# Reducing an angle in place in PSUM, and moving the split of a rotation's products between engines

## The chip, the cores and the metric

The kernel runs on one core of a Trainium2 chip. The metric is the device time of one execution in microseconds (us); of several runs the median counts. The core's engines are named as in the profile: PE (TensorE, matmul; PEld is its weight load), DVE (VectorE), ACT (ScalarE), POOL (GpSimd) and SP (SyncE, which issues the DMAs). Each engine works through its own instructions in order, and waits at an instruction until what that one needs is there. SBUF is the on-chip memory that all engines reach. PSUM is the memory that PE writes to, in 8 banks of 128 x 512 float32. In this kernel GpSimd only touches SBUF.

## The reference

Cut to what matters here; before it stands a clustered attention over 2 batches, 8 heads and 768 tokens, whose result is `x` of 2 x 768 x 512.

```
x = x + (relu(x.T @ w_tok1) @ w_tok2).T        # mixes tokens
x = x + relu(x @ w_ch1) @ w_ch2                # mixes channels, width 1536
theta = x @ w_theta                            # the rotation
zr, zi = x * cos(theta), x * sin(theta)
y = w_tok_r @ zr + w_tok_i @ zi                # over the tokens of one batch
u = x + y
out = u + relu(u @ w_ch)
```

Inputs are float32 or float64, and the products are kept to float32 accuracy.

## The kernel before

Every float32 operand of a product is split into two parts of the type float32r, x = h + l. One product is then three matmuls, l*h, h*l and h*h (`mm3`, L116 to L122), and each operand that is made on the chip has to be split first: h is a copy of x, l is x - h. `split_ps` (L86) splits from PSUM, with the copy on ACT and the subtraction on DVE. `split_sb` (L75) splits from SBUF with the engines that its last two arguments name: the copy by POOL ("p"), DVE ("v") or ACT ("a"), the subtraction by POOL ("p") or DVE ("v").

Tokens stand in 12 tiles of 128, six of each batch; `xn[t]` is tile t, 128 x 512, in SBUF. After the attention come the channel mixing and the rotation. The last third of the channel width (from L666) goes in three groups `ch` of four token tiles. For a group, `up` is called four times and `down` once for each of its tiles, and `advance()` is called after each of these, which is a tick. On these ticks a list `plan` runs the rotation of tiles that are done: `x2_turn(t)` transposes the tile and splits it, two ticks later `theta(t)` multiplies it by w_theta into a PSUM bank and `angle(t)` follows, one tick later `trig(t)`, and one more later `products(t)`. `up` ends with a split by ACT (L623) and DVE (L624), and `down` with an addition to `xn[t]` on DVE (L631), which `x2_turn` of that tile needs.

The angle is reduced by its whole turns before the sine. `angle` computes n = theta / 2 pi + MAGIC on ACT (L593), takes MAGIC off on DVE (L594), which leaves a rounded integer, and subtracts n times 2 pi in two steps on DVE (L595, L596), from PSUM into an SBUF tile r. `trig` takes |r| on ACT (L603), clips r on DVE (L604), and takes two sines on ACT (L605 for the cosine, L606 for the sine). `products` multiplies both by `xn[t]` and splits them: the cosine with DVE (L613), DVE (L80) and POOL (L84), the sine with POOL (L613), ACT (L82) and DVE (L84).

The last phase goes by `mix(t, b)`: 36 matmuls over the twelve split products z of one batch's six tiles, then an addition to xn on DVE (L698). One step later `u3_turn` transposes and splits the result, and a step after that `finish` multiplies it by w_ch and stores. The order of the steps begins (0,0), (1,0), (0,1), (2,0): the third is the first that needs tiles 6 to 11. `load_w` brings in each weight piece in between: a DMA, two ACT, two DVE (L105, L106) and a POOL instruction (L109), and a split whose subtraction is on POOL (L84).

PSUM banks of this part come from one pool of 8 (`bank`); SBUF tiles for the angle come from a pool of 8 with the tag "trig". The order of the instructions on each engine is set by the compiler, which simulates the program when it lays out the queues; the order in the source is the priority.

Of the kernel before, what the change touches and what calls it, by code (L numbers as in the profile page):

```python
# [18 lines left out]
P = 128  # L19
# [6 lines left out]
# How each chunk of the turned softmax is split: A by ScalarE and VectorE, B with GpSimd's difference, C by  # L26
# ScalarE's copy and GpSimd.
# [19 lines left out]
ZR = "va"  # L47
ZS = "pv"
# [3 lines left out]
def tile_model(ctx: ExitStack, tc: tile.TileContext, qT, kT, v, cent, w1, w2, wc1, wc2, wth, wri, wch, out):  # L52
    """Every float32 operand of a product is split exactly, x = h + l, into two float32r parts of 12
    significant bits; h*h + h*l + l*h are three one-pass products, accumulated in float32."""
    nc = tc.nc
    B, H, D, S = qT.shape
    NT = S // P          # token tiles of one batch
    NH = S // 2          # half of a row of scores: one PSUM bank
# [4 lines left out]
    NTT = w2.shape[1]    # tiles of the token-mixing width  # L63
# [10 lines left out]
    # ---------------------------------------------------------------- splits  # L74
    def split_sb(h, l, x, rnd, sub):  # L75
        """h, l <- x (SBUF), by the engines named."""
        if rnd == "p":
            nc.gpsimd.tensor_scalar(out=h, in0=x, scalar1=1.0, scalar2=0.0, op0=ALU.mult, op1=ALU.add)
        elif rnd == "v":
            nc.vector.tensor_copy(out=h, in_=x)  # L80
        else:
            nc.scalar.activation(out=h, in_=x, func=AF.Copy)  # L82
        e = nc.gpsimd if sub == "p" else nc.vector
        e.tensor_tensor(out=l, in0=x, in1=h.bitcast(F32), op=ALU.subtract)  # L84
# [8 lines left out]
    def load_w(src, name, pool=None):  # L93
        """A piece of a weight, [128, 512] float64, rounded to float32 and split."""
        raw = wpool.tile([P, 512, 2], U32, tag="wraw", bufs=3, name=f"{name}_raw")
        nc.sync.dma_start(out=raw.rearrange("p n t -> p (n t)"), in_=src.bitcast(U32))
        lo, hi = raw[:, :, 0], raw[:, :, 1]
        # The high word as a float32 has 3 bits of the exponent in its fraction; times 2^-112 is its
        # exponent in float32's bias. Shifted by 3 those fields are float32's, and the low word's top
        # bits, rounded, complete the fraction.  # L100
        w = wpool.tile([P, 512], F32, tag="wf", bufs=2, name=f"{name}_f")
        nc.scalar.activation(out=w, in_=hi.bitcast(F32), func=AF.Copy, scale=2.0**-112)
        nc.scalar.activation(out=lo, in_=lo, func=AF.Copy, scale=2.0**-29)
        wu = w.bitcast(U32)
        nc.vector.tensor_scalar(out=hi, in0=wu, scalar1=3, scalar2=None, op0=ALU.logical_shift_left)  # L105
        nc.vector.scalar_tensor_tensor(  # L106
            out=wu, in0=wu, scalar=0x80000000, in1=hi, op0=ALU.bitwise_and, op1=ALU.bitwise_or
        )
        nc.gpsimd.tensor_tensor(out=wu, in0=wu, in1=lo, op=ALU.add)  # L109
        pool, n = (pool, 12) if pool else (blk, WG)  # L110
        h, l = (pool.tile([P, 512], F32R, tag="wg", bufs=n, name=f"{name}_{k}") for k in "hl")
        split_sb(h, l, w, "pa"[wcount[0] % 2], "p")
        wcount[0] += 1
        return h, l

    def mm3(ps, pairs, first, last):  # L116
        """ps (+)= sum over the split pairs (lhsT, rhs) of lhsT.T @ rhs."""
        n = len(pairs)
        for i, ((ah, al), (bh, bl)) in enumerate(pairs):
            nc.tensor.matmul(ps, ah, bl, start=first and i == 0, stop=False)  # L120
            nc.tensor.matmul(ps, al, bh, start=False, stop=False)  # L121
            nc.tensor.matmul(ps, ah, bh, start=False, stop=last and i == n - 1)  # L122

    # ------------------------------------------------------------- attention
    with ExitStack() as actx:
# [10 lines left out]
        # Products of zeros keep the tensor engine's clock up.  # L136
# [8 lines left out]
        # Normalized centroids, placed for the products with two heads at a time.  # L145
# [9 lines left out]
        # One Newton step makes the root exact to float32.  # L155
# [9 lines left out]
        # cst[:, pair, 96 + 16 j + c]: two heads' centroids. The 128 columns from 96 - 32 i place their  # L165
        # products in rows 32 i ..
# [18 lines left out]
        # ltri.T @ x: of each row, the sum of the rows before it in its block of 16  # L185
# [12 lines left out]
        # one-hot rows of queries stay, those of keys become 0 (same cluster) or -BIG  # L198
# [11 lines left out]
        def masks(b, pr):  # L210
            """Cluster rows of two heads, 16 j .. for head j: one-hot of the queries' halves in rows 0 .. and
            32 .., of the keys' in 64 .. and 96 .. In steps, to go between other work."""
# [11 lines left out]
            # The factor 1 / (|q| + eps) of a row is positive and moves no maximum over the clusters.  # L224
# [17 lines left out]
            # Of equal maxima the first counts: the one with none before it.  # L242
# [26 lines left out]
        def prep_first(b, h):  # L269
            """Operands of a head: scores = [qh; qh].[kh; kl] + [ql; one-hot].[kh; mask]."""  # L270
# [35 lines left out]
        def split_pair(b, pr, ts):  # L306
            """Two heads' queries and keys, split."""
            parts = []
            for x, f, k in zip(ts, (scale, 1.0), "qk"):
                hi, lo = (ap.tile([P, S], F32R, tag="hl", bufs=HL, name=f"{k}{j}{b}{pr}") for j in "hl")  # L310
                if f != 1.0:
                    nc.gpsimd.tensor_scalar(out=x, in0=x, scalar1=f, scalar2=0.0, op0=ALU.mult, op1=ALU.add)
                split_sb(hi, lo, x, "p", "p")
                parts += [hi, lo]
            pairs[b, pr] = parts
# [3 lines left out]
        def place(i, m):  # L319
            """The cluster rows of head i of a pair."""  # L320
# [7 lines left out]
        def prep(b, h, m):  # L328
            """Operands of a head: scores = [qh; qh].[kh; kl] + [ql; one-hot].[kh; mask]."""
# [16 lines left out]
        def scores(b, h, u, ops):  # L346
            """Two tiles of queries: their softmax's numerators."""
# [22 lines left out]
        def turn(b, h, u, es):  # L370
            """Numerators with the keys on partitions, split."""
# [23 lines left out]
        def values(b, h, u, pr, vs):  # L395
            """[vh | vl].T @ (ph + pl); the halves' sum is the head's output, transposed."""
# [15 lines left out]
        def tokens(b, half):  # L412
            """x += relu(x.T @ w1) @ w2 for half of the channels, in 12 pieces."""
# [43 lines left out]
        def natural(b, pr):  # L457
            """Two heads' output with the tokens on partitions, divided by the softmax's sums."""
# [95 lines left out]
    # ------------------------------------------------------------------ mixers  # L554
    # channels: u + relu(u @ wc1) @ wc2
# [19 lines left out]
    def x2_turn(t):  # L575
        """x2 with the channels on partitions, split."""
        ps = bank(f"x2t{t}")
        for c in range(NC):
            nc.tensor.transpose(ps[:, c * P : c * P + P], xn[t][:, c * P : c * P + P], ident)
        h, l = block(f"x2h{t}"), block(f"x2l{t}")  # L580
        split_ps(h, l, ps)
        x2s[t] = h, l
# [6 lines left out]
    def angle(t):  # L589
        """theta less its whole turns."""  # L590
        th = ths.pop(t)
        n, r = (blk.tile([P, 512], F32, tag="trig", bufs=8, name=f"{k}{t}") for k in "nr")
        nc.scalar.activation(out=n, in_=th, func=AF.Copy, scale=INV2PI, bias=MAGIC)  # L593
        nc.vector.tensor_scalar(out=n, in0=n, scalar1=-MAGIC, scalar2=None, op0=ALU.add)  # L594
        nc.vector.scalar_tensor_tensor(out=r, in0=n, scalar=-C1, in1=th, op0=ALU.mult, op1=ALU.add)  # L595
        nc.vector.scalar_tensor_tensor(out=r, in0=n, scalar=-C2, in1=r, op0=ALU.mult, op1=ALU.add)  # L596
        trigs[t] = r

    def trig(t):
        """The angle's cosine, sin(pi/2 - |r|), and sine."""  # L600
        r = trigs[t]
        ra = blk.tile([P, 512], F32, tag="trig", bufs=8, name=f"ra{t}")
        nc.scalar.activation(out=ra, in_=r, func=AF.Abs)  # L603
        nc.vector.tensor_scalar(out=r, in0=r, scalar1=PI_LO, scalar2=-PI_LO, op0=ALU.min, op1=ALU.max)  # L604
        nc.scalar.activation(out=ra, in_=ra, func=AF.Sin, bias=halfpi, scale=-1.0)  # L605
        nc.scalar.activation(out=r, in_=r, func=AF.Sin)  # L606
        trigs[t] = ra, r

    def products(t):
        """x2's products with the cosine and the sine, split."""  # L610
        z = []
        for k, (tr, e) in enumerate(zip(trigs.pop(t), (nc.vector, nc.gpsimd))):
            e.tensor_tensor(out=tr, in0=tr, in1=xn[t], op=ALU.mult)  # L613
            zh, zl = block(f"zh{t}{k}"), block(f"zl{t}{k}")
            split_sb(zh, zl, tr, ZR[k], ZS[k])
            z.append((zh, zl))
        zs[t] = z
# [25 lines left out]
    # The last of the channels' width goes by groups of token tiles, with the rotation of the groups  # L643
    # that are done in between.
# [39 lines left out]
    # tokens again, then u + relu(u @ wch)  # L684
# [95 lines left out]
```

## Time and profile before

| What | Value |
|---|---|
| Runs, us | 704.73, 708.43, 709.75 (median 708.43) |
| Profiled execution: span, us | 707.2 |
| PE busy, us (share of the span) | 664.1 (94%) |
| DVE busy | 467.5 (66%) |
| POOL busy | 394.9 (56%) |
| ACT busy | 361.3 (51%) |
| HBM over the span | 62 GB/s |

The profile has no time of its own for the profiled execution but its span, from the first to the last instruction; it lies 1.2 us below the median of the runs and within their spread. Busy shares are means over the whole span: the attention, the channel mixing, the rotation and the last mixing have different loads, and rows of a stretch are read below.

### The profile page before, as it was taken

The page shows a single profiled execution, that of the slowest core. Times are in us where ns is not written, and L with a number is a line of the kernel's source. Part 1 is how long each engine was busy: PE and PEld are TensorE (multiplying, and loading weights), DVE is VectorE, ACT ScalarE, POOL GpSimd, SP SyncE. Part 2 cuts the span into 40 slices and gives each one's busy share as a digit, 9 for nine tenths or more (in the row PEclk, how much of TensorE's full clock was granted, in tenths as well). Part 3 has the DMA queues.
Part 4 walks back from the last instruction along what each step waited for, and adds up shares of the span by engine and source line. Part 5 has one row for each costly group of instructions (what it writes and reads, how often), then busy time and mean ns, then how long its engine had stood idle before and what let it go on. Part 6 is the DMA issues. An engine that isn't in the chain of part 4 may idle for free.

```text
span 707.2 us, 10584 instructions
## 1 busy us (share of the span) xinstructions
PE 664.1 (94%) x3772; PEld 580.9 (82%) x3772; DVE 467.5 (66%) x734; ACT 361.3 (51%) x698; POOL 394.9 (56%) x376
## 2 busy tenths in 40 slices
PE   7898888989999999999999999999996968999998
PEld 4798788888999999888888888888885846888886
DVE  6889888868788878376664432449799996433122
ACT  3687878687868786255533420435565444321000
POOL 7977789586838563348865520604476777433000
PEclk9999999999999999999999999999998999999999
DMA  8645645485434500013442310300011313320001
GB/s 259 159 89 156 172 106 144 100 246 141 90 85 104 121 19 1 1 50 130 150 149 60 120 59 1 107 14 1 31 44 45 93 55 109 101 89 16 31 30 45
DMA packets 24533, 62.27 MB, mean 88 GB/s; under 512 B 4320, under 2 KB 7584, under 8 KB 24480
## 3 DMA queue, kind: packets, MB, share of 16 engines
q1 hardware_dynamic: 24480, 61.59, 31.4%
q8 instruction: 30, 0.49, 0.3%
q14 instruction: 23, 0.19, 0.1%
HBM read 40.44 MB, written 3.15 MB: 62 GB/s over the span
## 4 chain that ended last, share of the span: by engine, by line
PE 71%; DVE 14%; DMA 4%; ACT 3%; issue 3%; SPq 2%; POOL 2%; ACTq 0%; DVEq 0%; POOLq 0%
PE o L401 7%; PE t L378 6%; PE r L120 4%; PE r L121 4%; PE r L122 4%; PE c L121 4%; PE c L122 4%; PE c L120 4%; PE y L120 4%; PE y L121 4%; PE y L122 4%; PE s L356 4%; PE s L357 3%; DMA w_raw<-w 3%; PE po L120 2%
## 5 line engine op out<-in xcount | busy, mean ns | idle before, releaser
L361 DVE TENSOR_REDUCE nm<-s 128x1 f32<-128x768 f32 x96 | 90.9, 948 | 18.0 <-PE s L357 17.4
L363 ACT ACTIVATE e<-s,nm 128x768 f32<-128x768 f32 x96 | 86.9, 905 | 22.4 <-DVE nm L361 11.8
L378 PE MATMUL t<-ident,e 128*128 128x128 f32 x576 | 81.6, 277 | 6.4 <-DVE pl L88 5.2
L356 PE MATMUL s<-k,qh 128*128 128x384 f32 x192 | 70.8, 369 | 8.6 <-ACT e L363 6.3
L401 PE MATMUL o<-ph,vs 128*128 128x256 f32 x288 | 76.0, 295 | 2.5 <-DVE xt L408 2.5
L378 PEld LDWEIGHTS t<-ident,e 128*128 128x128 f32 x576 | 68.7, 143 | 11.5 <-DVE pl L88 4.9
L401 PE MATMUL o<-pl,vs 128*128 128x256 f32 x288 | 73.6, 288 | 0.0
L88 DVE TENSOR_TENSOR pl<-t,ph 128x512 fp32r<-128x512 f32 x96 | 62.9, 678 | 6.7 <-ACT ph L87 5.1
L357 PE MATMUL s<-k,q 128*128 128x384 f32 x192 | 65.9, 344 | 1.3 <-ACT k L254 1.3
L87 ACT ACTIVATE ph<-t 128x512 fp32r<-128x512 f32 x96 | 54.9, 598 | 19.6 <-PE t L378 16.0
L389 POOL TENSOR_TENSOR pl<-pr,ph 128x512 fp32r<-128x512 f32 x48 | 62.7, 1306 | 2.0
L388 POOL TENSOR_SCALAR ph<-pr 128x512 fp32r<-128x512 f32 x48 | 30.6, 638 | 56.5 <-ACT pr L384 50.4
L401 PEld LDWEIGHTS o<-ph,vs 128*128 128x128 f32 x288 | 54.9, 191 | 3.9 <-DVE xt L408 3.5
L120 PE MATMUL y<-zl,k_h 128*128 128x512 f32 x144 | 56.9, 397 | 0.0
L121 PE MATMUL y<-zh,k_l 128*128 128x512 f32 x144 | 56.8, 394 | 0.0
L120 PE MATMUL r<-ul,c_h 128*128 128x512 f32 x144 | 56.7, 394 | 0.0
L121 PE MATMUL c<-c_h,rl 128*128 128x512 f32 x144 | 56.4, 393 | 0.2 <-DVE rl L624 0.2
L122 PE MATMUL y<-zh,k_h 128*128 128x512 f32 x144 | 56.5, 392 | 0.0
L122 PE MATMUL c<-c_h,rh 128*128 128x512 f32 x144 | 56.4, 393 | 0.0
L121 PE MATMUL r<-uh,c_l 128*128 128x512 f32 x144 | 56.0, 389 | 0.0
L120 PE MATMUL c<-c_l,rh 128*128 128x512 f32 x144 | 56.0, 396 | 0.0
L122 PE MATMUL r<-uh,c_h 128*128 128x512 f32 x144 | 55.9, 389 | 0.0
(201 smaller groups left out, 1718.1 us busy)
## 6 DMA issues: line engine op xcount, KB each, us to landing
c_raw<-wc SPq DMA_DIRECT2D x24, 512.0 KB, 3.4
k_raw<-wri SPq DMA_DIRECT2D x18, 512.0 KB, 3.7
qh<-qh SPq DMA_DIRECT2D x28, 192.0 KB, 3.0
k<-kh SPq DMA_DIRECT2D x28, 192.0 KB, 3.8
ql<-qT SPq DMA_DIRECT2D x8, 384.0 KB, 4.2
kl<-kT SPq DMA_DIRECT2D x8, 384.0 KB, 4.5
vr<-v SPq DMA_DIRECT2D x16, 192.0 KB, 3.2
w_raw<-w SPq DMA_DIRECT2D x6, 512.0 KB, 4.3
```

Of the source, the lines that this page charges most:

```text
L87: nc.scalar.activation(out=h, in_=ps, func=AF.Copy)
L88: nc.vector.tensor_tensor(out=l, in0=ps, in1=h.bitcast(F32), op=ALU.subtract)
L120: nc.tensor.matmul(ps, ah, bl, start=first and i == 0, stop=False)
L121: nc.tensor.matmul(ps, al, bh, start=False, stop=False)
L122: nc.tensor.matmul(ps, ah, bh, start=False, stop=last and i == n - 1)
L356: nc.tensor.matmul(ps[:, half, :NH], qh[:, c], k1[:, n], start=True, stop=False)
L357: last = nc.tensor.matmul(ps[:, half, :NH], ql[:, c], kk[:, n], start=False, stop=True)
L361: nc.vector.tensor_reduce(out=nm, in_=ps[:, :, :NH], axis=AX.XY, op=ALU.max, negate=True)
L363: nc.scalar.activation(out=e.rearrange("p (a n) -> p a n", a=2), in_=ps[:, :, :NH], func=AF.Exp, bias=nm, accum_out=sums[b, h // 2][:, qt, ...
L378: nc.tensor.transpose(ps[:, a, i * P : i * P + P], es[i][:, kt * P : kt * P + P], ident)
L389: nc.gpsimd.tensor_tensor(out=pl, in0=raw, in1=ph.bitcast(F32), op=ALU.subtract)
L401: nc.tensor.matmul(ps[:, :256], vs[:, kt, :], p[:, kt % 2, :], start=n == 0 and k == 0, stop=n == NT - 1 and k == 1,)
```

## The change

The angle is no longer brought to an SBUF tile. MAGIC is taken off on ACT. Both subtractions write back into theta's own PSUM bank, |r| and the clip read from there, and the first of the two sines, the cosine, is written over it. DVE multiplies the cosine by x2 in the bank, and `split_ps` splits it from there: copy on ACT, subtraction on DVE. The bank is held until that subtraction has read it. The sine keeps its product on POOL and its copy on ACT; its subtraction goes from DVE to POOL, and the cosine's subtraction from POOL to DVE. Comments are dropped as well; nothing else is changed.

```diff
     def angle(t):
-        th = ths.pop(t)
-        n, r = (blk.tile([P, 512], F32, tag="trig", bufs=8, name=f"{k}{t}") for k in "nr")
+        th = ths[t]
+        n = blk.tile([P, 512], F32, tag="trig", bufs=8, name=f"n{t}")
         nc.scalar.activation(out=n, in_=th, func=AF.Copy, scale=INV2PI, bias=MAGIC)
-        nc.vector.tensor_scalar(out=n, in0=n, scalar1=-MAGIC, scalar2=None, op0=ALU.add)
-        nc.vector.scalar_tensor_tensor(out=r, in0=n, scalar=-C1, in1=th, op0=ALU.mult, op1=ALU.add)
-        nc.vector.scalar_tensor_tensor(out=r, in0=n, scalar=-C2, in1=r, op0=ALU.mult, op1=ALU.add)
-        trigs[t] = r
+        nc.scalar.activation(out=n, in_=n, func=AF.Copy, bias=-MAGIC)
+        nc.vector.scalar_tensor_tensor(out=th, in0=n, scalar=-C1, in1=th, op0=ALU.mult, op1=ALU.add)
+        nc.vector.scalar_tensor_tensor(out=th, in0=n, scalar=-C2, in1=th, op0=ALU.mult, op1=ALU.add)

     def trig(t):
-        r = trigs[t]
-        ra = blk.tile([P, 512], F32, tag="trig", bufs=8, name=f"ra{t}")
-        nc.scalar.activation(out=ra, in_=r, func=AF.Abs)
-        nc.vector.tensor_scalar(out=r, in0=r, scalar1=PI_LO, scalar2=-PI_LO, op0=ALU.min, op1=ALU.max)
-        nc.scalar.activation(out=ra, in_=ra, func=AF.Sin, bias=halfpi, scale=-1.0)
+        th = ths.pop(t)
+        ra, r = (blk.tile([P, 512], F32, tag="trig", bufs=8, name=f"{k}{t}") for k in ("ra", "r"))
+        nc.scalar.activation(out=ra, in_=th, func=AF.Abs)
+        nc.vector.tensor_scalar(out=r, in0=th, scalar1=PI_LO, scalar2=-PI_LO, op0=ALU.min, op1=ALU.max)
+        nc.scalar.activation(out=th, in_=ra, func=AF.Sin, bias=halfpi, scale=-1.0)
         nc.scalar.activation(out=r, in_=r, func=AF.Sin)
-        trigs[t] = ra, r
+        trigs[t] = th, r

     def products(t):
-        z = []
-        for k, (tr, e) in enumerate(zip(trigs.pop(t), (nc.vector, nc.gpsimd))):
-            e.tensor_tensor(out=tr, in0=tr, in1=xn[t], op=ALU.mult)
-            zh, zl = block(f"zh{t}{k}"), block(f"zl{t}{k}")
-            split_sb(zh, zl, tr, ZR[k], ZS[k])       # ZR = "va", ZS = "pv"
-            z.append((zh, zl))
-        zs[t] = z
+        co, r = trigs.pop(t)
+        (ch, cl), (sh, sl) = ((block(f"z{j}{t}{k}") for j in "hl") for k in range(2))
+        nc.vector.tensor_tensor(out=co, in0=co, in1=xn[t], op=ALU.mult)
+        split_ps(ch, cl, co)
+        nc.gpsimd.tensor_tensor(out=r, in0=r, in1=xn[t], op=ALU.mult)
+        split_sb(sh, sl, r, "a", "p")
+        zs[t] = [(ch, cl), (sh, sl)]
```

## Rows read from the trace of the kernel before

**Rows 1.** Busy us by stretch: length, PE, PEld, DVE, ACT, POOL; then granted clock, DMA.

```profile
480.00:500.00 20.00, 20.00 (x92) 16.41 (x92) 18.17 (x27) 10.45 (x18) 9.59 (x7) 1.00 0.00 1
...
515.00:531.50 16.50, 16.35 (x72) 13.08 (x71) 16.43 (x20) 8.96 (x17) 11.68 (x9) 1.00 0.20 64
531.50:541.40 9.90, 4.07 (x13) 3.22 (x12) 9.16 (x13) 3.95 (x7) 5.93 (x5) 0.66 0.17 53
541.40:571.40 30.00, 30.00 (x138) 24.50 (x136) 27.09 (x33) 16.45 (x30) 22.95 (x17) 1.00 0.23 70
571.40:589.30 17.90, 8.62 (x30) 6.89 (x30) 15.52 (x18) 8.16 (x15) 14.02 (x10) 0.81 0.21 60
...
600.00:640.00 40.00, 40.00 (x186) 33.15 (x185) 15.74 (x23) 11.12 (x18) 18.68 (x17) 1.00 0.29 89
```

**Rows 2.** Timeline of PE: start us, us, instruction, then idle before it and releaser.

```profile
537.59 1.12 PE L579 MATMUL x2t<-ident,xn 128*128 128x128 f32 x4 [5.83 <-DVE xn L631]
...
541.42 0.39 PE L121 MATMUL c<-c_h,rl 128*128 128x512 f32 x1
541.64 0.39 PE L122 MATMUL c<-c_h,rh 128*128 128x512 f32 x1
...
546.58 0.60 PE L579 MATMUL x2t<-ident,xn 128*128 128x128 f32 x4
546.94 0.47 PE L120 MATMUL th<-th_l,x2h 128*128 128x512 f32 x1
...
575.57 1.12 PE L703 MATMUL u<-ident,xn 128*128 128x128 f32 x4 [4.11 <-DVE xn L698]
...
578.97 0.40 PE L120 MATMUL y<-zl,k_h 128*128 128x512 f32 x1
...
586.36 1.12 PE L703 MATMUL u<-ident,xn 128*128 128x128 f32 x4 [5.17 <-DVE xn L698]
...
589.28 0.39 PE L120 MATMUL y<-zl,k_h 128*128 128x512 f32 x1
```

**Rows 3.** Timeline of DVE from 515 us: an early instruction and two additions.

```profile
515.64 0.68 DVE L88 TENSOR_TENSOR x2l<-x2t,x2h 128x512 fp32r<-128x512 f32 x1
...
536.86 1.28 DVE L631 TENSOR_TENSOR xn<-c,xn 128x512 f32<-128x512 f32 x2
...
574.84 0.68 DVE L698 TENSOR_TENSOR xn<-y,xn 128x512 f32<-128x512 f32 x1
```

**Rows 4.** Groups of DVE by line, 466 to 590 us: count, busy us, mean ns.

```profile
L84 DVE TENSOR_TENSOR zl<-r,zh 128x512 fp32r<-128x512 f32 x12 | 15.5, 1296 | 2.5 <-ACT zh L82 2.5
L613 DVE TENSOR_TENSOR ra<-ra,xn 128x512 f32<-128x512 f32 x12 | 14.3, 1191 | 2.0 <-ACT ra L605 1.9
L596 DVE SCALAR_TENSOR_TENSOR r<-n,r 128x512 f32<-128x512 f32 x12 | 10.9, 908 | 0.3
L594 DVE TENSOR_SCALAR n<-n 128x512 f32<-128x512 f32 x12 | 9.8, 816 | 3.8 <-ACT n L593 3.8
L80 DVE CAST zh<-ra 128x512 fp32r<-128x512 f32 x12 | 8.4, 703 | 0.1
L604 DVE TENSOR_SCALAR r<-r 128x512 f32<-128x512 f32 x12 | 8.0, 665 | 1.4 <-ACT ra L603 1.4
```

**Rows 5.** Single lines, 466 to 590 us: shortest, median and longest in ns.

```profile
L594 DVE TENSOR_SCALAR n<-n x12: 411/424/1536, 472.0 to 569.3; 128x512 f32<-128x512 f32 x12
...
L595 DVE SCALAR_TENSOR_TENSOR r<-n,th x12: 671/677/690, 473.1 to 571.3; 128x512 f32<-128x512 f32 x12
...
L613 DVE TENSOR_TENSOR ra<-ra,xn x12: 676/1104/1798, 477.8 to 579.2; 128x512 f32<-128x512 f32 x12
L613 POOL TENSOR_TENSOR r<-r,xn x12: 1287/1583/1746, 478.3 to 580.4; 128x512 f32<-128x512 f32 x12
...
L84 POOL TENSOR_TENSOR zl<-ra,zh x12: 1268/1404/1695, 482.8 to 585.1; 128x512 fp32r<-128x512 f32 x12
```

**Rows 6.** Groups of ACT by line, 466 to 590 us: count, busy us, mean ns.

```profile
L82 ACT ACTIVATE zh<-r 128x512 fp32r<-128x512 f32 x12 | 7.5, 624 | 9.6 <-POOL r L613 9.6
...
L87 ACT ACTIVATE x2h<-x2t 128x512 fp32r<-128x512 f32 x11 | 6.5, 593 | 3.1 <-PE x2t L579 3.1
```

More of the change, by code (lines that the diff above doesn't have):

```diff
@@ L46 @@
 WARM = (17, 4, 20, 18)
-ZR = "va"
-ZS = "pv"
 @with_exitstack
@@ L589, in angle @@
     def angle(t):
-        th = ths.pop(t)
-        n, r = (blk.tile([P, 512], F32, tag="trig", bufs=8, name=f"{k}{t}") for k in "nr")
-        nc.scalar.activation(out=n, in_=th, func=AF.Copy, scale=INV2PI, bias=MAGIC)
-        nc.vector.tensor_scalar(out=n, in0=n, scalar1=-MAGIC, scalar2=None, op0=ALU.add)
-        nc.vector.scalar_tensor_tensor(out=r, in0=n, scalar=-C1, in1=th, op0=ALU.mult, op1=ALU.add)
-        nc.vector.scalar_tensor_tensor(out=r, in0=n, scalar=-C2, in1=r, op0=ALU.mult, op1=ALU.add)
@@ L597, in angle @@
-        trigs[t] = r
-    def trig(t):
-        r = trigs[t]
-        ra = blk.tile([P, 512], F32, tag="trig", bufs=8, name=f"ra{t}")
-        nc.scalar.activation(out=ra, in_=r, func=AF.Abs)
-        nc.vector.tensor_scalar(out=r, in0=r, scalar1=PI_LO, scalar2=-PI_LO, op0=ALU.min, op1=ALU.max)
-        nc.scalar.activation(out=ra, in_=ra, func=AF.Sin, bias=halfpi, scale=-1.0)
+        th = ths[t]
+        n = blk.tile([P, 512], F32, tag="trig", bufs=8, name=f"n{t}")
+        nc.scalar.activation(out=n, in_=th, func=AF.Copy, scale=INV2PI, bias=MAGIC)
@@ new lines, in angle, with trig @@
+        nc.scalar.activation(out=n, in_=n, func=AF.Copy, bias=-MAGIC)
+        nc.vector.scalar_tensor_tensor(out=th, in0=n, scalar=-C1, in1=th, op0=ALU.mult, op1=ALU.add)
+        nc.vector.scalar_tensor_tensor(out=th, in0=n, scalar=-C2, in1=th, op0=ALU.mult, op1=ALU.add)
+    def trig(t):
+        th = ths.pop(t)
+        ra, r = (blk.tile([P, 512], F32, tag="trig", bufs=8, name=f"{k}{t}") for k in ("ra", "r"))
+        nc.scalar.activation(out=ra, in_=th, func=AF.Abs)
+        nc.vector.tensor_scalar(out=r, in0=th, scalar1=PI_LO, scalar2=-PI_LO, op0=ALU.min, op1=ALU.max)
+        nc.scalar.activation(out=th, in_=ra, func=AF.Sin, bias=halfpi, scale=-1.0)
```

## The prediction

> **What bounds the kernel now.** I read the busy times first. PE is busy for 664.1 of 707.2 us, so the place to look is where it isn't. Busy times by stretch show that inside the rotation: PE is full up to 531 us, then has 4.07 of 9.90 us and 8.62 of 17.90 us in two stretches around a full one, and is full again afterwards [rows 1]. The timeline of PE says what it waits for. Three times it stands before a group of transposes: 5.83 us for the addition of L631, 4.11 us and 5.17 us for that of L698 [rows 2]. That is 15.11 us. Each addition is one DVE instruction of under 0.7 us that only needs a finished matmul; it is late because DVE has other work queued ahead of it. DVE is busy for 16.43 of 16.50 us, 9.16 of 9.90, 27.09 of 30.00 and 15.52 of 17.90 us in these stretches, while ACT and POOL have room [rows 1]. So in this part DVE's queue sets the end.
>
> After each wait PE also runs slower for a while: the granted clock of the two stretches with waits is 0.66 and 0.81, against 1.00 in the full ones, which is a mix of the two levels, 1.2 and 2.4 GHz [rows 1]. From 537.59 to 541.42 us it starts a group of four transposes and seven matmuls. At full clock the transposes take 0.36 us (546.58 to 546.94) and a matmul starts every 0.23 us (541.42 to 541.64), so this should be 0.36 + 7 x 0.23 = 1.97 us; it is 3.83, and 1.86 us is lost. After the second wait (575.57 to 578.97, six matmuls) it is 3.40 - 1.74 = 1.66 us, after the third (586.36 to 589.28, five) 2.92 - 1.51 = 1.41 us [rows 2]. In all 4.93 us. **The waits and the slow clock behind them are worth 15.11 + 4.93 = 20.0 us.** No other stall of PE in the rotation or the last mixing is as long, and DVE is 90% busy at 480 to 500 us as well, with PE full [rows 1], so work that DVE saves there buys nothing.
>
> Why DVE is so slow shows in the spread of single lines. L595, which reads theta in PSUM, takes 671 to 690 ns in all twelve cases. L594 has both operands in SBUF and takes 411 to 1536 ns, L613 with two SBUF inputs 676 to 1798 [rows 5]. DVE's SBUF work is stretched while POOL works, its PSUM work isn't.
>
> **DVE's part.** Per tile DVE now spends 1.296 + 1.191 + 0.908 + 0.816 + 0.703 + 0.665 us on L84, L613, L596, L594, L80 and L604 [rows 4] and 0.677 on L595 [rows 5]: 6.26 us. The change leaves two subtractions, the clip, the cosine's product and its l part: five instructions, each with one PSUM input. I price each at 0.677 us, the median of L595: 3.39 us. **DVE saves 2.87 us per tile.** Three of the five now write to PSUM, which no row of DVE shows. Its cost lies between 0.671 us, the shortest of L595 (a shorter one is not expected, since the shortest two-input row with everything in SBUF is 0.676), and twice the price, 1.354 us, should read and write in one bank exclude each other [rows 5]. I take the lower end, because the nearest row already streams the same 512 elements from PSUM.
>
> The saving against the three waits:
> - First wait. Between L88 at 515.64 and L631 at 536.86 us [rows 3] DVE runs almost without a pause, and 17 of its instructions there are the rotation's, at seven per tile 2.4 tiles. 2.4 x 2.87 = 6.9 us, so L631 starts at 530.0. PE arrives at 537.59 - 5.83 = 531.8 [rows 2]. The wait goes, with 1.8 us to spare.
> - Second wait. Up to L698 at 574.84 [rows 3] there are 21 such instructions from 541.4 us on, three tiles: 8.6 us, so 566.2. PE arrives at 571.5. The wait goes.
> - Third wait. By then all four last tiles are through, 11.5 us. The second L698 ends just before 586.36 and moves to about 575, PE arrives at 581.2. The wait goes.
>
> **ACT's part.** It gets two copies more per tile: MAGIC from SBUF at the price of L82, 0.624 us, and the cosine's h from PSUM at that of L87, 0.593 [rows 6]: 1.22 us, 4.9 us for the last four tiles. From 541.4 to 589.3 us it is busy for 24.6 of 47.9 us [rows 1], so the copies lie beside DVE's and PE's work. The cosine overwrites what the clip reads, so the sine of L605 now waits for DVE's clip. Behind it in ACT's queue stand the other sine, x2h, rh and the weights' copies; DVE, PE and POOL wait for those. If that cover is gone, the chain of a tile grows by the 1.22 us and as many as two handovers.
>
> **POOL's part.** Product and subtraction of the sine take the place of product and subtraction of one each: the count is the same, 1.58 + 1.40 us by the medians of its rows, with shortest ones of 1.287 and 1.268 [rows 5]. But the sine's way is now POOL, ACT, POOL, with a copy of 0.624 us [rows 6] for which POOL stands still if nothing else is queued. POOL is busy for 22.95 + 14.02 = 37.0 of the 47.9 us from 541.4 to 589.3 [rows 1]. Without the waits of PE that stretch lasts some 40 us, of which POOL fills 37. The stall that remains is therefore POOL's: between nothing and about 6 us, when its idle time of 10.9 us is kept to the half. I take 2.5 us, nearer to nothing, because POOL's own work is stretched too and shortens when DVE leaves SBUF. No DMA is added or moved; the loads behind these POOL instructions only follow their buffers.
>
> **The bank.** Theta's bank is now held until the cosine's l part is written, instead of until L595. Six instructions more of 0.6 to 0.7 us and their handovers make about 5 us, plus what they queue. The pool of eight covers it at the pace of one tile per 24 matmuls and a group of transposes, 24 x 0.23 + 0.36 = 5.9 us.
>
> **A rule against it.** The rows price an addition of a constant at 411 ns on DVE when undisturbed, 816 ns on average [rows 4, 5], and a copy on ACT at 624 [rows 6]. The Trainium skill, "ScalarE: Activation LUTs", Rules for kernel authors, says that additions and the like belong on VectorE and not on ScalarE; by it the move of MAGIC would cost 0.2 us of engine time per tile. The trace agrees only for an undisturbed DVE.
>
> **Sum.** 20.0 us less 2.5 us that remain: 17.5 us. The profiled span of 707.2 becomes 689.7 us; the median of the runs lies 1.2 us higher, 708.43 - 17.5 = 690.9. **I forecast 691 us.**
>
> **The rivals.**
> - POOL becomes the bound: it keeps its gaps, and the last tiles' sines and the next weights come about 6 us late, with some 1.5 us of slow clock behind, and perhaps a second time for less. 20 - 10 = 10 us gained: 698 us. For it: 37 of 40 us. Against it: only the sine needs POOL now.
> - PSUM writes are dear, 1.354 us for three instructions. The saving falls to 0.84 us per tile: L631 comes at 534.8 (3.0 us of the wait remain), the two L698 about 1 us late each, and the clock's 4.9 us stay: 20 - 9.9 = 10 us, 698 us.
> - The stretching stays with DVE. If POOL's accesses hold up DVE as long as before, only at other instructions (L105, L106), what counts is the undisturbed price: three at the 0.411 us of the shortest L594 and four at 0.677 [rows 5] are 3.94 us, a saving of 0.55 per tile. Then 4.5, 2.4 and 2.9 us of the waits and all of the clock's cost remain, 5.3 us are gained: 703 us. The Trainium skill, "VectorE: DVE Perf Modes", Rules for kernel authors, points this way: who has many operations to do on a matmul's output should copy it out of PSUM first. Against it: L595 isn't stretched once in twelve.
> - Slower: PE runs out of banks. If so many banks hold angles that each group of matmuls has to wait for the evacuation of the one before, ACT 0.593 and DVE 0.677 us [rows 5, 6], the some 30 groups of this part lose 30 x 1.27 = 38 us: 691 + 38 = 729 us. This begins when six of eight banks hold angles, at a hold of 6 x 5.9 = 35 us in the even part. The new chain needs about a quarter of that; only the last four tiles, whose thetas follow each other closely, come near, with two mixes and a transpose beside them.
> - The compiler lays the queues out anew, and the additions stand behind other work again: no change, 708 us.
>
> **How the numbers follow.** Forecast 0.63 (687 to 695), POOL 0.14, dear writes 0.07, stretching stays 0.06, out of banks 0.05, no change 0.05. The runs before spread by 0.7%, so a change of 1% is about what can be told: faster is below 701.3 us, slower above 715.5. Faster: 0.63 + 0.14 + 0.07 and a part of the stretching, 0.86; same 0.09; slower 0.05. The range goes from 686 us (all 20 us gained, and a run at the low end of the spread) to 702.
>
> **What would show it.** After the change PE's idle time before L579 and L703 should be below 1 us each and the granted clock 1.00 throughout these stretches; the five DVE lines should stand at 0.67 to 0.69 us with almost no spread; DVE should be busy for about two thirds of the stretch and POOL for over 85%; L698 should start within 1 us of its matmul. The prediction is wrong if PSUM writes show above 0.8 us, if PE waits with a release from POOL's l parts or from a bank, or if DVE stays over 90% busy with L105 and L106 stretched.

## The result and the profile after

The changed kernel takes 690.99 us in the median of 4 runs (689.80 to 692.06), against 708.69 us of 4 runs before. The ratio is 0.9759, with a 95% interval of 0.9725 to 0.9792. The forecast was 691. The profiled execution spans 690.2 us, 17.0 us less than before. Two constants went and `angle` got a line shorter, so the lines behind them have lower numbers now: the addition of `down` is L628 (it was L631), that of `mix` L695 (L698), the transposes L577 and L700 (L579 and L703), `split_ps` L85 and L86.

Busy times by stretch of the changed kernel, with the columns of [rows 1]:

```profile
515.00:531.50 16.50, 16.50 (x77) 13.68 (x76) 14.42 (x24) 14.13 (x26) 12.48 (x11) 1.00 0.30 95
531.50:541.40 9.90, 8.30 (x44) 6.71 (x43) 7.36 (x10) 7.49 (x14) 7.70 (x8) 1.00 0.01 2
541.40:571.40 30.00, 28.35 (x129) 22.97 (x128) 22.75 (x34) 23.21 (x42) 25.20 (x21) 1.00 0.36 105
571.40:589.30 17.90, 17.90 (x82) 14.83 (x81) 10.77 (x14) 5.76 (x10) 13.68 (x12) 1.00 0.41 127
```

PE has 4.07 of 9.90 and 8.62 of 17.90 us no more [rows 1], but 8.30 and 17.90, and the granted clock of these stretches is 1.00 instead of 0.66 and 0.81. DVE comes down from 27.09 to 22.75 us in the long stretch, ACT rises from 16.45 to 23.21, POOL from 22.95 to 25.20 because more of its work now falls into that stretch.

The timeline of PE, every instruction of the rotation before which it waited for 0.2 us or more:

```profile
536.43 0.50 PE L118 MATMUL th<-th_l,x2h 128*128 128x512 f32 x1 [1.60 <-ACT x2h L85]
...
569.31 0.66 PE L700 MATMUL u<-ident,xn 128*128 128x128 f32 x4 [0.54 <-DVE xn L695]
571.08 0.47 PE L118 MATMUL po<-ch_l,u3h 128*128 128x512 f32 x1 [1.11 <-ACT u3h L85]
```

Of the 15.11 us of waits in [rows 2] 3.25 us are left, 11.9 us less, and with the 4.9 us of slow clock behind them this makes 16.8 of the 17.0 us. What is left is mostly not DVE's any more: 2.71 us are released by ACT.

The rotation's five DVE instructions, as groups by line from 466 to 590 us, with the weights' L103 and L104 (k and ch are two weights) beside them (columns as in [rows 4]):

```profile
L104 DVE SCALAR_TENSOR_TENSOR k_f<-k_f,k_raw 128x512 uint32<-128x512 uint32 x11 | 9.1, 831 | 0.7
L103 DVE TENSOR_SCALAR k_raw<-k_f 128x512 uint32<-128x512 uint32 x11 | 8.5, 776 | 10.5 <-ACT k_f L100 10.5
L610 DVE TENSOR_TENSOR th<-th,xn 128x512 f32<-128x512 f32 x12 | 8.3, 695 | 6.3 <-ACT th L602 6.3
L594 DVE SCALAR_TENSOR_TENSOR th<-n,th 128x512 f32<-128x512 f32 x12 | 8.3, 691 | 0.2
L593 DVE SCALAR_TENSOR_TENSOR th<-n,th 128x512 f32<-128x512 f32 x12 | 8.3, 688 | 1.0 <-ACT n L592 1.0
L601 DVE TENSOR_SCALAR r<-th 128x512 f32<-128x512 f32 x12 | 8.2, 686 | 4.9 <-ACT ra L600 4.8
L86 DVE TENSOR_TENSOR zl<-th,zh 128x512 fp32r<-128x512 f32 x12 | 8.2, 683 | 0.9 <-ACT zh L85 0.9
...
L104 DVE SCALAR_TENSOR_TENSOR ch_f<-ch_f,ch_raw 128x512 uint32<-128x512 uint32 x4 | 4.4, 1100 | 0.3
```

All five stand at 683 to 695 ns, the three that write to PSUM (L593, L594, L610) hardly above the others. Per tile that is 3.44 us, against 6.26 before [rows 4, 5].

That it is POOL's work beside them that stretches DVE's SBUF operations shows in the trace of the kernel before. Of the 36 instructions of L613, L84 and L596, 13 overlap no instruction of POOL, and these all take 0.68 or 0.69 us; of the other 23, twenty take 0.94 to 1.80 us. Two of L613, the first beside POOL's work and the second not, and what POOL did:

```profile
519.74 1.78 DVE L613 TENSOR_TENSOR ra<-ra,xn 128x512 f32<-128x512 f32 x1
...
530.33 0.68 DVE L613 TENSOR_TENSOR ra<-ra,xn 128x512 f32<-128x512 f32 x1
```

```profile
519.56 1.41 POOL L84 TENSOR_TENSOR zl<-ra,zh 128x512 fp32r<-128x512 f32 x1 [0.36 <-DVE zh L80]
520.93 1.75 POOL L613 TENSOR_TENSOR r<-r,xn 128x512 f32<-128x512 f32 x1
...
528.71 1.41 POOL L84 TENSOR_TENSOR zl<-ra,zh 128x512 fp32r<-128x512 f32 x1 [0.36 <-DVE zh L80]
531.68 1.41 POOL L109 TENSOR_TENSOR k_f<-k_f,k_raw 128x512 uint32<-128x512 uint32 x1 [1.56 <-DVE k_f L106]
```

In the changed kernel 38 of the 60 instructions of the five lines overlap POOL's work for 0.4 us or more, and none takes over 0.70 us. On POOL the two instructions of the sine have become shorter as well, 1.31 and 1.33 us on average:

```profile
L82 POOL TENSOR_TENSOR zl<-r,zh 128x512 fp32r<-128x512 f32 x12 | 15.9, 1325 | 7.1 <-ACT zh L80 5.3 <-DVE zl L86 1.8
L612 POOL TENSOR_TENSOR r<-r,xn 128x512 f32<-128x512 f32 x12 | 15.7, 1308 | 27.7 <-ACT r L603 27.7
```

**A length to compare by.** The work ahead of the rotation has the same source in nearly all the kernels below, but reaches the first theta anywhere from 465.3 to 469.5 us. So beside the times I give the length from the first theta (the first start of its weight load) to the last `finish` (the last start of its first matmul). It is one profiled execution for each kernel, read from the views of the tiles th and po, for the kernel before:

```profile
L120 PEld LDWEIGHTS th<-th_l,x2h x48: 187/188/190, 468.2 to 554.8; 128*128 128x128 f32 x48
...
L120 PE MATMUL po<-ch_l,u3h x52: 278/393/775, 587.1 to 703.5; 128*128 128x512 f32 x44, 128*128 128x256 f32 x8
```

and after:

```profile
L118 PEld LDWEIGHTS th<-th_l,x2h x48: 186/188/190, 468.2 to 548.0; 128*128 128x128 f32 x48
...
L118 PE MATMUL po<-ch_l,u3h x52: 278/393/474, 571.1 to 686.5; 128*128 128x512 f32 x44, 128*128 128x256 f32 x8
```

703.5 - 468.2 = 235.3 us, and 686.5 - 468.2 = 218.3 us.

### The profile page after: what moved, and what is told of

It reads as the page before. It is cut to its first block, busy times and chain, and to the rows that moved or that the text cites. A ratio compares the mean times of both kernels' runs of the same rounds, so it can differ in the third digit from the quotient of the medians.

```text
span 690.2 us, 10585 instructions
## 1 busy us (share of the span) xinstructions
PE 659.0 (95%) x3772; PEld 578.1 (84%) x3772; DVE 436.5 (63%) x710; ACT 372.8 (54%) x722; POOL 387.2 (56%) x376
## 4 chain that ended last, share of the span: by engine, by line
PE 74%; DVE 6%; DMA 6%; ACT 5%; POOL 4%; issue 3%; SPq 2%; ACTq 0%; POOLq 0%; DVEq 0%
PE o L399 7%; PE t L376 6%; PE r L118 5%; PE r L119 5%; PE r L120 5%; PE c L118 5%; PE c L119 5%; PE c L120 5%; PE y L120 4%; PE y L118 4%; PE y L119 4%; PE s L354 3%; PE s L355 3%; DMA w_raw<-w 3%; ACT e L361 2%
## 5 line engine op out<-in xcount | busy, mean ns | idle before, releaser
L359 DVE TENSOR_REDUCE nm<-s 128x1 f32<-128x768 f32 x96 | 90.9, 949 | 20.9 <-PE s L355 20.3
L86 DVE TENSOR_TENSOR pl<-t,ph 128x512 fp32r<-128x512 f32 x96 | 62.9, 678 | 6.5 <-ACT ph L85 4.8
L85 ACT ACTIVATE ph<-t 128x512 fp32r<-128x512 f32 x96 | 54.9, 598 | 17.6 <-PE t L376 14.8
L399 PEld LDWEIGHTS o<-pl,vs 128*128 128x128 f32 x288 | 56.1, 195 | 0.5 <-POOL pl L387 0.5
```

The costliest lines, as they stand in the source:

```text
L85: nc.scalar.activation(out=h, in_=ps, func=AF.Copy)
L86: nc.vector.tensor_tensor(out=l, in0=ps, in1=h.bitcast(F32), op=ALU.subtract)
L359: nc.vector.tensor_reduce(out=nm, in_=ps[:, :, :NH], axis=AX.XY, op=ALU.max, negate=True)
L399: nc.tensor.matmul(ps[:, :256], vs[:, kt, :], p[:, kt % 2, :], start=n == 0 and k == 0, stop=n == NT - 1 and k == 1,)
```

## The experiments

The theory: PE waited for single additions behind DVE's queue, and the change shortens that queue, partly by moving work and partly because operands in PSUM aren't stretched by POOL. The rivals: only the moves count; only the compiler's new order counts; and for what is left, POOL is the next bound, or ACT is. All kernels start from the changed one. PE's waits in the table are those of 0.2 us or more within the rotation.

| Kernel | Median, us | Ratio to before (95%) | Rotation, us | PE's waits in it, us |
|---|---|---|---|---|
| before | 708.69 | | 235.3 | 15.11 |
| the change | 690.99 | 0.9759 (0.9725 to 0.9792) | 218.3 | 3.25 |
| e1_sbuf | 705.00 | 0.9941 (0.9922 to 0.9960) | 232.0 | 11.24 |
| e2_magic_dve | 685.51 | 0.9667 (0.9642 to 0.9692) | 214.5 | 0 |
| e3_sine_sub_dve | 693.37 | 0.9774 (0.9746 to 0.9802) | 220.2 | 3.60 |
| e4_dve_4 | 699.31 | 0.9871 (0.9838 to 0.9904) | 226.5 | 8.95 |
| e5_act_1 | 687.56 | 0.9690 (0.9659 to 0.9721) | 216.0 | 1.11 |
| e6_pool_1 | 690.89 | 0.9732 (0.9695 to 0.9770) | 217.6 | 2.40 |
| e7_act_2 | 697.37 | 0.9824 (0.9793 to 0.9855) | 223.1 | 5.07 |
| e8_banks_6 | 692.70 | 0.9771 (0.9731 to 0.9811) | 217.7 | 2.58 |
| e9_x2h_dve | 689.68 | 0.9740 (0.9714 to 0.9765) | 218.1 | 3.25 |
| e10_magic_dve (e2 again) | 687.13 | 0.9697 (0.9670 to 0.9724) | 214.4 | 0 |
| e11_act_1 (e5 again) | 689.11 | 0.9723 (0.9698 to 0.9747) | 216.4 | 1.51 |
| e12_change (the change again) | 691.70 | 0.9755 (0.9731 to 0.9779) | 218.0 | 2.85 |

The first four kernels ran on one chip, the next four on one, the last four on one, each beside runs of the kernel before (medians 708.60, 709.23 and 708.70 us).

**The same engines, but in SBUF (e1_sbuf).**

```diff
-    scalar_tensor_tensor(out=th, in0=n, scalar=-C1, in1=th, ...)      # DVE
-    scalar_tensor_tensor(out=th, in0=n, scalar=-C2, in1=th, ...)
+    scalar_tensor_tensor(out=r, in0=n, scalar=-C1, in1=th, ...)       # r: SBUF tile
+    scalar_tensor_tensor(out=r, in0=n, scalar=-C2, in1=r, ...)
     # trig: Abs and the clip read r; the cosine goes to the SBUF tile ra, and products works on ra
```

> Every operation stays on the engine that the change gave it, but the angle, the cosine and its product live in SBUF tiles as before the change, and PSUM holds theta only until the first subtraction. Queue theory (what counts is how long DVE's queue is ahead of the additions, and SBUF operands stretch it): DVE needs 0.68 + 0.91 + 0.67 + 1.19 + 1.30 = 4.74 us a tile at the durations of before, a saving of 1.5 instead of 2.9 us, so about 2 us of the first wait and its slow clock come back and the other two waits stay away: 695 us (693 to 698), with DVE's SBUF lines between 0.42 and 1.8 us. Rival, only the moves between engines count: 691 us, as the change. Rival, the compiler's new order did it: any time from 691 to 708 us, without relation to DVE's busy time.

The groups of its DVE:

```profile
L611 DVE TENSOR_TENSOR ra<-ra,xn 128x512 f32<-128x512 f32 x12 | 14.0, 1163 | 2.1 <-ACT ra L603 2.0
L86 DVE TENSOR_TENSOR zl<-ra,zh 128x512 fp32r<-128x512 f32 x12 | 13.9, 1158 | 2.3 <-ACT zh L85 2.1
L594 DVE SCALAR_TENSOR_TENSOR r<-n,r 128x512 f32<-128x512 f32 x12 | 11.9, 991 | 0.4
L602 DVE TENSOR_SCALAR r<-r 128x512 f32<-128x512 f32 x12 | 8.5, 705 | 0.2
...
L593 DVE SCALAR_TENSOR_TENSOR r<-n,th 128x512 f32<-128x512 f32 x12 | 8.1, 676 | 1.5 <-ACT n L592 1.5
```

and the waits on its PE's timeline:

```profile
535.23 1.11 PE L577 MATMUL x2t<-ident,xn 128*128 128x128 f32 x4 [4.38 <-DVE xn L629]
541.54 0.50 PE L119 MATMUL th<-th_h,x2l 128*128 128x512 f32 x1 [0.27 <-DVE x2l L86]
...
571.36 0.66 PE L701 MATMUL u<-ident,xn 128*128 128x128 f32 x4 [2.09 <-DVE xn L696]
...
577.51 0.50 PE L118 MATMUL y<-zl,k_h 128*128 128x512 f32 x1 [1.15 <-DVE zl L86]
...
581.82 0.80 PE L118 MATMUL y<-zl,k_h 128*128 128x512 f32 x1 [3.35 <-DVE zl L86]
```

DVE's cost per tile is 0.676 + 0.991 + 0.705 + 1.163 + 1.158 = 4.69 us, as expected (4.74). The time isn't: 705 instead of 695 us. The moves alone give 3.3 us of the rotation; what lives in PSUM is all that the sources of e1 and of the change differ in, and with it comes the rest, 13.7 us. The rival that only the moves count is out. POOL gains by it too: its product and its subtraction of the sine take 1.53 and 1.46 us on average in e1, 1.31 and 1.33 in the change. But half of the saved DVE time has bought a fifth of the gain, so my way of setting the saving against each wait is too simple: the additions are still late by 4.38 and 2.09 us, and PE now also waits for the l part of the cosine itself, 4.5 us, which DVE makes in this kernel and POOL made before. The rival that the compiler's order makes part of the 13.7 us isn't excluded: its range, 691 to 708 us, holds the result, and that of the queue theory doesn't.

**MAGIC back on DVE (e2_magic_dve).**

```diff
-    nc.scalar.activation(out=n, in_=n, func=AF.Copy, bias=-MAGIC)
+    nc.vector.tensor_scalar(out=n, in0=n, scalar1=-MAGIC, scalar2=None, op0=ALU.add)
```

> The change with one part undone: MAGIC is taken off by DVE again, from SBUF. Queue theory: DVE gets 0.4 to 0.8 us a tile back, a saving of 2.0 to 2.4 us a tile, less than 1 us of the first wait returns: 691 to 694 us. Rival, the waits that are left (1.60 and 1.11 us, both released by ACT) come from ACT's two added copies: without one of them they shrink, 689 us.

This is the fastest of all, 685.5 us and 3.8 us less of rotation than the change. Its busy times by stretch (columns as in [rows 1]):

```profile
515.00:541.40 26.40, 26.40 (x124) 21.73 (x124) 24.25 (x39) 18.84 (x34) 20.74 (x18) 1.00 0.19 62
541.40:589.30 47.90, 47.90 (x219) 39.68 (x218) 31.36 (x47) 26.89 (x47) 38.40 (x30) 1.00 0.37 107
```

PE is full throughout, at full clock; no wait of 0.2 us is left in the rotation. From 235.3 to 214.5 us it has gained 20.8 us, close to the 20.0 us at which the prediction put all waits with their slow clock. DVE pays 0.88 us on average for the instruction that it has got back, and it makes nothing late. The queue theory's 691 to 694 us failed. The rival, ACT's added copies, had the direction right; its 689 us was still too high.

**The sine's subtraction back on DVE (e3_sine_sub_dve).**

```diff
-    split_sb(sh, sl, r, "a", "p")
+    split_sb(sh, sl, r, "a", "v")
```

> The change with one part undone: the sine's l part is subtracted by DVE again, from SBUF, and no longer by POOL. Queue theory: DVE gets 0.7 to 1.3 us a tile back, POOL loses 1.3; a saving of 1.6 to 2.2 us a tile on DVE, 0 to 2 us of the first wait return: 692 to 695 us. Rival, POOL is the bound of the changed kernel: its relief makes this faster than the change, 688 us.

693.4 us. The interval of the ratio overlaps the change's; the rotation is 1.9 us longer than with the change. DVE's new line costs 0.93 us a tile; the addition of L695 is late by 2.35 us again:

```profile
569.60 0.81 PE L700 MATMUL u<-ident,xn 128*128 128x128 f32 x4 [2.35 <-DVE xn L695]
```

POOL's relief doesn't make it faster.

**DVE's load put back (e4_dve_4).**

```diff
     split_ps(ch, cl, co)
+    for _ in range(4):
+        nc.vector.tensor_tensor(out=d, in0=co, in1=xn[t], op=ALU.add)     # d is never read
```

> The change, and behind each cosine's split four more DVE instructions from the bank into an unused SBUF tile, 4 x 0.68 = 2.7 us a tile, about what the change saves on DVE. They add nothing to the result. Queue theory: DVE's load is that of before, its additions are late again and PE waits for them: 703 to 709 us. Rival, the gain came from less contention for SBUF or a shorter chain per tile and not from DVE's load: 691 to 695 us.

699.3 us: nearly half of the gain is gone, not all of it, and the queue theory's 703 to 709 us missed. The one big wait of PE isn't for an addition:

```profile
541.61 0.79 PE L118 MATMUL th<-th_l,x2h 128*128 128x512 f32 x1 [8.37 <-ACT x2h L85]
```

and ACT's timeline shows what stood ahead of x2h in its queue:

```profile
532.15 0.67 ACT L101 ACTIVATE ch_raw<-ch_raw 128x512 uint32<-128x512 uint32 x1 [3.89 <-DMA ch_raw<-wch]
...
539.96 0.60 ACT L85 ACTIVATE zh<-th 128x512 fp32r<-128x512 f32 x1 [2.86 <-DVE th L610]
540.45 0.62 ACT L80 ACTIVATE zh<-r 128x512 fp32r<-128x512 f32 x1
540.97 1.08 ACT L85 ACTIVATE x2h<-x2t 128x512 fp32r<-128x512 f32 x2
```

ACT waits for a load, then for DVE's product, and only then copies x2h. So DVE's load counts where something that PE needs is queued behind it, here through ACT. That the gain has nothing to do with DVE's load is out: 691 to 695 us was its range.

**ACT's time or the chain's length (e5_act_1, then e10, e11 and e12 side by side).** e5 is e2 with a copy on ACT, in `angle`, that nothing waits for:

```diff
     nc.vector.tensor_scalar(out=n, in0=n, scalar1=-MAGIC, scalar2=None, op0=ALU.add)
+    nc.scalar.activation(out=d, in_=xn[t], func=AF.Copy)                  # d is never read
```

> The kernel with MAGIC back on DVE, and where ACT took MAGIC off in the change one copy of x2 by ACT into an unused SBUF tile, 0.62 us a tile that nothing waits for. It adds nothing to the result. If ACT's time is what MAGIC on ACT costs: back to the changed kernel, 689 to 691 us, with waits of PE released by ACT (x2h, u3h). If it is the longer chain of a tile (two ACT copies in a row before DVE may begin): stays at 685 to 686 us.

> The kernel with MAGIC back on DVE once more, on the same chip as the next two, to part ACT's time from the chain's length: 685 to 686 us.

> MAGIC on DVE, and 0.62 us a tile on ACT that nothing waits for. If its distance to the one before is that of the changed kernel, all of the loss is ACT's time; if it is nothing, all is the chain; the first look put it at 2 of 5.5 us, so 687 to 688.

> The changed kernel itself, on the same chip as the three before: 690 to 692 us.

Both times the kernel with the idle copy lies between the other two: 214.5 and 214.4 us of rotation with MAGIC on DVE, 216.0 and 216.4 with the copy added, 218.3 and 218.0 with the change. The ends are clearly apart on one chip (0.9670 to 0.9724 against 0.9731 to 0.9779), the middle one's interval reaches into both. In both, PE waits for x2h again, in e5:

```profile
533.09 0.50 PE L118 MATMUL th<-th_l,x2h 128*128 128x512 f32 x1 [1.11 <-ACT x2h L85]
```

So ACT's time alone can cost 1.5 to 2.0 us where the compiler put the idle copies. That isn't MAGIC's place: they need only xn, and in e5 and e11 four of the twelve run before the first theta and four close to x2h. So how the 3.7 us divide into ACT's time, the longer chain of the tile and the order that the compiler makes of it, I can't tell.

**More POOL, more ACT (e6_pool_1, e7_act_2).**

```diff
+    nc.gpsimd.tensor_tensor(out=d, in0=r, in1=xn[t], op=ALU.add)          # e6, behind the sine's split
+    for _ in range(2): nc.scalar.activation(out=d, in_=co, func=AF.Copy)  # e7, behind the cosine's split
```

> The change, and behind each sine's split one more product on POOL into an unused SBUF tile, 1.3 us a tile. It adds nothing to the result. If POOL is the next bound, as the prediction said (37 of some 40 us busy): the last sines and the next weights come later by up to 4 x 1.3 us, 694 to 697 us, with waits of PE on POOL's l parts. If ACT is the next bound: 690 to 692 us.

> The change, and behind each cosine's split two more copies by ACT from the bank into an unused SBUF tile, 1.2 us a tile, about what the change itself added on ACT. They add nothing to the result. If ACT is the next bound: PE's waits for x2h and u3h grow from 2.7 us to 5 or more, 694 to 698 us. If POOL is: 690 to 692 us.

1.3 us a tile more on POOL cost nothing: 690.9 us. One wait for POOL appears, 0.88 us for a weight's l part:

```profile
537.37 0.50 PE L118 MATMUL th<-th_l,x2h 128*128 128x512 f32 x1 [1.52 <-ACT x2h L85]
...
584.46 0.51 PE L119 MATMUL y<-zh,k_l 128*128 128x512 f32 x1 [0.88 <-POOL k_l L82]
```

1.2 us a tile more on ACT cost 4.8 us of rotation, and the wait for x2h doubles:

```profile
537.55 0.80 PE L118 MATMUL th<-th_l,x2h 128*128 128x512 f32 x1 [3.53 <-ACT x2h L85]
```

ACT's queue is the next thing to be late, and POOL's isn't. e7 also holds the bank some 1.2 us longer; the next kernel shows that banks aren't short.

**Six banks (e8_banks_6).** The pool `ps_m` has 6 banks instead of 8.

> The change with a pool of 6 PSUM banks instead of 8 from the channel mixing on. If the longer hold of theta's bank is covered, as the prediction has it (a hold of some 15 us at one tile per 5.9 us takes 2 to 3 banks, up to 4 for the last four tiles): 690 to 693 us. Rival, banks are short: PE waits before thetas and mixes for the evacuation of a bank, 697 us or more.

The rotation takes 217.7 us, as with the change, and PE's three waits are those for x2h, xn and u3h. The longer hold of theta's bank costs nothing, with two banks to spare. (The profiled execution took 696.2 us, the slowest of the four, and begins its rotation only at 473.2 us. It lost that in the attention, where this pool isn't used yet: from 120 to 180 us it gets 357 matmuls done at a granted clock of 0.91, the change 385 at 0.97.)

**x2h by DVE (e9_x2h_dve).**

```diff
     # x2_turn
-    split_ps(h, l, ps)                                   # copy on ACT
+    nc.vector.tensor_copy(out=h, in_=ps)
+    nc.vector.tensor_tensor(out=l, in0=ps, in1=h.bitcast(F32), op=ALU.subtract)
```

> The change, with the copy h of x2_turn's split made by DVE and no longer by ACT. If what is left of PE's waits comes from x2h standing behind other work in ACT's queue: the wait of 1.6 us before a theta goes, 688 to 690 us. If it is the compiler's order or the length of the tile's chain: 691 us or, since DVE gets 0.68 us a tile more, 692.

689.7 us; its interval covers the change's ratio, so nothing is gained that can be told. The wait changes its owner:

```profile
535.81 0.50 PE L118 MATMUL th<-th_l,x2h 128*128 128x512 f32 x1 [1.52 <-DVE x2h L579]
...
569.87 0.66 PE L701 MATMUL u<-ident,xn 128*128 128x128 f32 x4 [1.73 <-DVE xn L696]
```

DVE's queue is as late with x2h as ACT's was, and late with an addition besides. A single copy moved from one late queue to another brings nothing here; e2, which takes MAGIC off ACT's queue in all twelve tiles, does.

## Why the prediction was right, and where it wasn't

**The bound** was read rightly. The waits for L631 and L698 were 15.11 us, the slow clock behind them 4.93, together 20.0; e2 and e10, where PE doesn't wait at all, gain 20.8 and 20.9 us of rotation.

**DVE's price** was right: 0.677 us each forecast, 0.683 to 0.695 measured, writes to PSUM included; 2.82 us saved per tile instead of 2.87. The rival of dear PSUM writes is out. The waits for the additions went from 15.11 to 0.54 us. Of the signs that were named, PE's idle time before L577 and L700 (none, and 0.54 us), the clock of 1.00 and the five lines (0.676 to 0.700 us in all sixty cases) came; from 541.4 to 589.3 us DVE is busy for 70%, near the two thirds, but POOL for 81% and not over 85%.

**The size of each wait's end** I worked out by moving the addition forward by the DVE time saved ahead of it. It gave the right answer for the change because there was room to spare, if less than the 1.8 us named for the first wait: PE needs the end of the addition, 0.68 us after its start. (For the second wait 22 instructions of DVE stand in the trace and not 21; nothing hangs on it.) e1 shows that it doesn't hold in general: the same arithmetic gave 695 us, and 705 was measured. Which instruction waits behind which changes with the compiler's order, and an operand of PE that DVE makes now, here the cosine's l part, can come late itself.

**ACT's part** is the step that failed. "The copies lie beside DVE's and PE's work" was argued from ACT's busy share, 24.6 of 47.9 us. In fact one of the two, MAGIC's, costs 3.6 to 3.8 us (e2 against the change, e10 against e12): without it PE's waits for x2h, which I had named among what stands behind the copies, and for u3h are gone. The timeline of ACT in the changed kernel shows what x2h stands behind:

```profile
532.07 0.67 ACT L101 ACTIVATE ch_raw<-ch_raw 128x512 uint32<-128x512 uint32 x1 [1.58 <-DMA ch_raw<-wch]
...
535.26 0.63 ACT L80 ACTIVATE zh<-r 128x512 fp32r<-128x512 f32 x1 [0.39 <-POOL r L612]
535.80 0.58 ACT L85 ACTIVATE x2h<-x2t 128x512 fp32r<-128x512 f32 x1
```

It stands 1.58 us for a load of a weight that is only needed for `finish`, and works through five instructions more, before it copies x2h, for which PE waits until 536.43. None of the five is a MAGIC copy: they are the two sines and the two copies zh of a tile, and a weight's copy. In e2 the sines and copies of that tile are through before the load's copy, and x2h follows it at once:

```profile
528.36 0.69 ACT L602 ACTIVATE th<-ra,halfpi 128x512 f32<-128x512 f32 x1 [1.45 <-DVE r L601]
...
531.84 0.67 ACT L101 ACTIVATE ch_raw<-ch_raw 128x512 uint32<-128x512 uint32 x1
532.41 0.58 ACT L85 ACTIVATE x2h<-x2t 128x512 fp32r<-128x512 f32 x1
```

So x2h is late here by way of the tile's later steps, which with MAGIC on ACT come behind the load. Whether the longer chain puts them there or the order that the compiler chose stays open.

**What remains** was put at 2.5 us and on POOL. It is 3.25 us, of which ACT releases 2.71. That the sum came out within 1 us is to that extent luck: the right size for the wrong reason. The reason was shaky by its own numbers. Without the two waits (9.28 us) and the slow clock behind them (3.07 us) the stretch of 47.9 us would last 35.6 us and not some 40, less than POOL's 37.0, so POOL should have been the bound. It wasn't: its instructions for the sine got shorter, and e6 fits 1.3 us a tile more into POOL, busy for 42.3 us from 541.4 to 589.3, without loss.

**The rule of the Trainium skill** against the move of MAGIC ("ScalarE: Activation LUTs", Rules for kernel authors: additions belong on VectorE) has the runs on its side, 685.5 us (e2) against 691.0. By engine time it doesn't look so: DVE pays 0.88 us in e2 for what costs ACT 0.62 in the change. The kernel is faster all the same, since PE's waits for ACT are gone.

**The other rule of the Trainium skill**, from "VectorE: DVE Perf Modes", Rules for kernel authors, which would copy a matmul's output out of PSUM first where many operations follow, is contradicted here: e1 brings the angle to SBUF with its first subtraction and takes 705 us against 691. Where the rival had a point is that some stretching stays: the weights' L104 for ch takes 1.10 us on average in the change (0.92 before, where it is L106), L103 for k 0.78 (0.58, L105).

**The bank** was right: e8 has no wait for one. The hold was sized too small, at about a quarter of 35 us: from the first matmul of a theta to the end of the cosine's subtraction it is 12 to 16 us for the first nine tiles and 22, 25 and 29 us for the last three. At most four banks hold angles at a time.

**The compiler's order** as the cause by itself fits badly. That repeated kernels agree within 0.4 us of rotation doesn't speak against it, since a repeat has the same order. But e6 and e9, whose queues are ordered otherwise than the change's, stay within 0.7 us of its rotation, while time added to DVE's queue (e4) or ACT's (e7) costs 8.2 and 4.8 us. It isn't excluded as a part of the 13.7 us of e1 and of the 3.7 us of MAGIC's move, since each edit changes the order too.

The version with MAGIC on DVE beats both kernels: 685.5 and 687.1 us in two sets of runs, ratios of 0.9667 and 0.9697.

## What to carry to other kernels

Where PE waits for one short instruction, look at what is queued ahead of it on its engine, and price that queue at the durations of the trace: what shares SBUF with POOL took up to 1.80 us here instead of 0.68, and keeping it in PSUM was worth more than moving it to another engine. Before a move, look at the receiving queue not for its busy share but for what stands behind the new instructions: an engine that is busy half of the time can still be late for the one copy that PE needs, above all when it also waits for loads. After a change that worked, undo its parts one by one; here one of them, MAGIC on ACT, cost 3.7 us, nearly a fifth of the 20.8 us that the others gain.

## What the runs showed of the hardware

DVE takes the same time for a float32 tile of 128 x 512 whether it writes PSUM or SBUF, as long as one operand is in PSUM: 0.688 and 0.691 us for the subtractions in place (L593, L594), 0.683 for the l part in SBUF. A tile was read and written in the same bank here, at that price.

The sine of L602 that ACT writes to PSUM takes 0.684 us on average, and the same sine into SBUF took 0.719 on average before and 0.716 in e1 (L603 there); a small gain. The granted clock of PE stayed at 1.00 through waits of 1.6 and 1.1 us in the change, and its mean is 0.66 and 0.81 in the stretches with waits of 4 to 6 us before [rows 1]. In e3 it fell to 0.50, the lower level, from 570.6 to 572.6 us, behind the wait of 2.35 us that ended at 569.60.
